# A routed feed-forward tail for short experts: rounded and rest columns side by side in one stationary operand

## The chip, the cores and the metric

The kernel runs on one core of a Trainium2 chip. The metric is the device time of one execution in microseconds, the median of several runs. Engines are named as the profile names them: PE is the matrix engine, PEld its weight load, DVE the vector engine, ACT the scalar engine, POOL the GpSimd engine, SP the engine that only issues transfers here. A name with a q behind it (DVEq, PEldq) is an engine's sequencer, which reads the program, branches and waits on semaphores.

## The reference

Three layers follow each other on 1536 tokens of 512 features. First local attention with pooled keys, then a dense feed-forward layer with 2048 hidden features, then the part that the change touches: eight experts of 1024 hidden features, of which each token uses one, up to 384 tokens for an expert.

```python
logits = x @ w_gate
expert_idx = np.argmax(logits, axis=1)
...
h = np.maximum(np.einsum('ecd,edf->ecf', disp, w1), 0.0)
y = np.einsum('ecf,efd->ecd', h, w2)
...
        out[i] = gate_w[i] * y[expert_idx[i], pos[i]]
```

Worked out from the reference with its own random seed, the experts get 880, 425, 168, 62 and 1 tokens, sorted by number; three experts get none.

## The kernel before

Attention and the dense layer take the first 370 us and are one long straight program. Then the experts run, sorted by their number of tokens, largest first; k is the place in that order. How many tokens each one has is known only while the kernel runs, so every engine loads the count into a register (count, line 1331) and branches on it.

Tokens are handled in blocks of 128. Experts with two or three blocks run through many_blocks; with one block through single (line 1353), which calls one_block (line 703). By the counts above k = 0 takes three blocks (the first is a special one), k = 1 three, k = 2 two, and k = 3 and k = 4 one block each. The places k = 3 and k = 4 are what this case is about.

Every matrix product is done in a 32-bit format with a shortened mantissa, and the lost part is made good: an operand is kept as a rounded value and the rest (its difference from the exact value), and a product is the sum of three passes, rounded by rounded, rounded by rest of the weights, rest by rounded weights (PASSES, line 662). In one_block the tokens are the stationary operand (128 columns) and 512 columns of weights move. The first layer is two halves of four chunks, so 2 x 4 x 3 = 24 matmuls (Block.first, line 671); ACT takes the positive part; PE turns the result by four 128x128 transposes per half (Block.turn, line 681), ACT and DVE make its rounded and rest parts; the second layer is 8 x 3 = 24 matmuls (Block.second, line 695); finish (line 646) scales by the gate and POOL scatters the rows to the output.

While a block runs, the weights of the next expert come in. They are 16 chunks of 256 KB. SP loads a chunk into one of eight raw buffers (raw_load, line 602); conv_hi (line 606) casts it to the rounded part, on ACT, or on DVE for chunks 2, 5, 8, 11 and 14; conv_lo (line 615) subtracts to get the rest, on DVE, or on POOL for those five chunks, and then lets SP load the chunk eight places on into the freed buffer. So chunk 15 can be loaded only when chunk 7 is converted. The call more(n) places the conversion of the next n chunks at that place of the program; each engine works its instructions off in program order, so a conversion that waits for its transfer holds up what stands behind it on that engine. In one_block the calls are 2, 3, 1, 1, then one after each of the second-layer steps 2 to 6, and what is left, four chunks, after finish. At step 4 ahead turns the next expert's gathered tokens (load_xT, line 637).

The branches around it are small (line 1378) for places with at most one block and large (line 1391) for the others. The code of the last alternative stands far behind that of the first, and what is not taken is jumped over.

## Time and profile before

| what | value |
|---|---|
| time, three runs | 508.5, 509.41 and 511.25 us, median 509.41 |
| the profiled execution's own time | 508.64 us |
| its span, first to last instruction | 506.9 us |
| mean granted PE clock | 0.981 |
| busy share of the span: PE, DVE, ACT, POOL | 93%, 64%, 54%, 37% |
| k = 3, first matmul to last (read from the timeline) | 472.36 to 485.22 us |
| k = 4, first matmul to last | 485.06 to 497.88 us |
| last scatter issued, end | 499.18, 506.9 us |

A matmul's row gives its start and a modelled end, and matmuls overlap: one of 512 columns is shown with some 0.39 us, while a row of them starts one every 0.23 to 0.24 us. The busy share of the whole span says little about the two short blocks, which are 5% of it; there the order of events is read from the timeline. A wait that is put down to "issue" is one for which the profile shows no cause; the rows of the sequencers around it show whether the engine was at a branch.

### The profile page before, as it was taken

The page shows a single profiled execution, that of the slowest core. Times are in us where ns is not written, and L with a number is a line of the kernel's source. Part 1 is how long each engine was busy: PE and PEld are TensorE (multiplying, and loading weights), DVE is VectorE, ACT ScalarE, POOL GpSimd, SP SyncE. Part 2 cuts the span into 40 slices and gives each one's busy share as a digit, 9 for nine tenths or more (in the row PEclk, how much of TensorE's full clock was granted, in tenths as well). Part 3 has the DMA queues.
Part 4 walks back from the last instruction along what each step waited for, and adds up shares of the span by engine and source line. Part 5 has one row for each costly group of instructions (what it writes and reads, how often), then busy time and mean ns, then how long its engine had stood idle before and what let it go on. Part 6 is the DMA issues. An engine that isn't in the chain of part 4 may idle for free.

```text
span 506.9 us, 9236 instructions
## 1 busy us (share of the span) xinstructions
PE 472.0 (93%) x3052; PEld 406.9 (80%) x3052; DVE 325.6 (64%) x880; ACT 271.8 (54%) x681; POOL 189.3 (37%) x197
## 2 busy tenths in 40 slices
PE   7798798889999999999999999999998999999892
PEld 6586577678888889999999899888767989888672
DVE  4699999878877761111149889846686755556460
ACT  4755656666667646664333333334654865566550
POOL 4345575633333335883223233223335040030440
PEclk9988998999999999999999999999999999999997
DMA  8996656667777441439010010012645966458380
GB/s 237 283 255 185 191 162 189 214 207 245 227 230 219 126 142 46 125 118 345 37 62 2 0 63 0 2 63 88 200 129 151 345 211 222 135 164 278 105 292 15
DMA packets 45634, 79.97 MB, mean 158 GB/s; under 512 B 4604, under 2 KB 19196, under 8 KB 45552
## 3 DMA queue, kind: packets, MB, share of 16 engines
q1 hardware_dynamic: 43792, 73.83, 46.4%
q0 software_dynamic: 1760, 5.19, 3.4%
q8 instruction: 34, 0.56, 0.5%
q14 instruction: 48, 0.39, 0.2%
HBM read 65.29 MB, written 13.11 MB: 155 GB/s over the span
## 4 chain that ended last, share of the span: by engine, by line
PE 65%; DVE 15%; DMA 13%; issue 2%; ACT 2%; POOL 1%; SPq 0%; DVEq 0%; POOLq 0%
PE acc L426 23%; PE h L393 22%; DMA xgq<-x2d,gidx 10%; PE bh L750 6%; PE y L739 5%; DMA vt<-vT 2%; DVE t1i L375 2%; DVE t1i L372 2%; DVE t1o L375 1%; DMA xg<-x2d,gidx 1%; PE T L294 1%; DVE st L285 1%; DVE sc L272 1%; PE O L334 1%; DVE t1o L372 1%
## 5 line engine op out<-in xcount | busy, mean ns | idle before, releaser
L393 PE MATMUL h<-xT,Wi 128*128 128x384 f32 x768 | 152.8, 346 | 8.2 <-DVE e L404 6.6
L393 PEld LDWEIGHTS h<-xT,Wi 128*128 128x128 f32 x768 | 137.2, 192 | 16.5 <-DVE e L404 8.7
L426 PE MATMUL acc<-Wo,g 128*128 128x512 f32 x576 | 145.8, 397 | 1.0 <-POOL Wo L382 1.0
L413 POOL TENSOR_TENSOR g<-e,g 128x384 fp32r<-128x384 f32 x63 | 71.4, 1133 | 145.5 <-ACT g L409 129.9
L426 PEld LDWEIGHTS acc<-Wo,g 128*128 128x128 f32 x576 | 105.9, 188 | 21.7 <-POOL Wo L382 1.3
L404 DVE SCALAR_TENSOR_TENSOR e<-e,h 128x384 f32<-128x384 f32 x64 | 35.3, 551 | 77.3 <-ACT e L400 77.3
L399 ACT ACTIVATE e<-h 128x384 f32<-128x384 f32 x64 | 31.4, 491 | 65.4 <-PE h L393 61.8
L409 ACT CAST g<-e 128x384 fp32r<-128x384 f32 x64 | 32.8, 513 | 42.6 <-DVE e L404 42.6
L618 DVE TENSOR_TENSOR E<-rawq,E 128x512 fp32r<-128x512 f32 x70 | 46.7, 705 | 9.1 <-ACT E L608 8.0
L279 ACT ACTIVATE sc<-sc,st 128x120 f32<-128x120 f32 x96 | 36.8, 385 | 28.8 <-DVE st L272 28.6
L750 PE MATMUL bh<-xbq,E 128*128 128x256 f32 (+1 forms) x288 | 43.6, 303 | 2.7 <-ACT ysf L654 1.4
L608 ACT CAST E<-rawq 128x512 fp32r<-128x512 f32 x75 | 42.7, 617 | 6.2 <-DMA rawq<-wx 3.5
L750 PEld LDWEIGHTS bh<-xbq,E 128*128 128x128 f32 x288 | 41.3, 188 | 5.0 <-ACT ysf L654 1.6
L287 POOL TENSOR_TENSOR sc<-sc,st 128x360 f32<-128x360 f32 x32 | 29.6, 925 | 41.3 <-DVE st L286 20.1
L739 PE MATMUL y<-E,g 128*128 128x512 f32 x168 | 41.7, 393 | 0.0
L488 DVE CUSTOM_DVE_ANT_0 dot<-a,wgb 128x512 f32<-128x512 f32 x48 | 40.0, 887 | 0.0
L739 PEld LDWEIGHTS y<-E,g 128*128 128x128 f32 x168 | 30.6, 188 | 5.7
L400 ACT ACTIVATE e<-e 128x384 f32<-128x384 f32 x64 | 33.7, 526 | 2.0
L272 DVE CUSTOM_DVE_ANT_0 sc<-S,masks 128x120 f32<-128x120 f32 x96 | 21.5, 276 | 14.2 <-PE S L247 10.4
L758 DVE TENSOR_TENSOR g<-e,g 128x256 fp32r<-128x256 f32 (+1 forms) x24 | 11.3, 469 | 23.8 <-ACT g L757 23.6
L655 POOL DMA_INDIRECT out<-ys,sidx x6 | 6.3, 1053 | 47.4 <-ACT ys L654 46.0
L755 ACT ACTIVATE e<-bh 128x256 f32<-128x256 f32 (+1 forms) x24 | 10.1, 419 | 22.4 <-PE bh L750 22.4
(225 smaller groups left out, 634.5 us busy)
## 6 DMA issues: line engine op xcount, KB each, us to landing
rawq<-wx SPq DMA_DIRECT2D x88, 256.0 KB, 4.3
rawi<-wi SPq DMA_DIRECT2D x16, 512.0 KB, 5.0
rawo<-wo SPq DMA_DIRECT2D x16, 512.0 KB, 5.5
vw<-vP SPq DMA_DIRECT2D x16, 288.0 KB, 6.7
kt<-kT SPq DMA_DIRECT2D x8, 400.0 KB, 5.6
qt<-qT SPq DMA_DIRECT2D x16, 192.0 KB, 5.9
vt<-vT SPq DMA_DIRECT2D x8, 384.0 KB
out<-xg SPq DMA_DIRECT2D x12, 256.0 KB, 3.6
```

Source lines behind the costliest of these rows:

```text
L279: nc.scalar.activation(out=sc[:, gi], in_=sc[:, gi], func=AF.Exp, bias=st[:, 0, gi : gi + 1], scale=-1.0, accum_out=st[:, 1, gi : gi + 1])
L393: nc.tensor.matmul(HP[t, f][:, 0:TT], lhsT=w[:, s, c * P : (c + 1) * P], rhs=xT[t][:, xs, c, :], start=c == 0 and n == 0, stop=c == NCC - ...
L400: nc.scalar.activation(out=e, in_=e, func=AF.Relu, bias=1.0, scale=-1.0)
L404: nc.vector.scalar_tensor_tensor(out=e, in0=e, scalar=-1.0, in1=h[:, 0:TT], op0=ALU.mult, op1=ALU.max)
L409: nc.scalar.copy(gT[t, f][:, 0], EP[t, f])
L413: eng.tensor_tensor(g[:, 1], EP.pop((t, f)), g[:, 0].bitcast(F32), op=ALU.subtract)
L426: nc.tensor.matmul(accp[tb], lhsT=g[:, s, tb * P : (tb + 1) * P], rhs=w[:, ws], start=f % FPG == 0 and n == 0, stop=f % FPG == FPG - 1 and ...
L488: nc.vector.tensor_tensor_reduce(out=junk, in0=x2[t * BPT + tb], in1=WGB[e // 2][:, e % 2], scale=1.0, scalar=0.0, op0=ALU.mult, op1=ALU.a ...
L608: (nc.vector.tensor_copy if m in vec else nc.scalar.copy)(EW[k][m][:, 0], raw_of(k, m))
L618: (nc.gpsimd if m in pool else nc.vector).tensor_tensor(w[:, 1], raw, w[:, 0].bitcast(F32), op=ALU.subtract)
L739: nc.tensor.matmul(ys[b], lhsT=g[:, s, b * P : (b + 1) * P], rhs=w[:, ws], start=f == 0 and n == 0, stop=f == 7 and n == 2)
L750: nc.tensor.matmul(h[:, 0:nt], lhsT=EW[k][half * NCC + c][:, ws, fc * P : (fc + 1) * P], rhs=xb[:, s, c, 0:nt], start=n == 0, stop=n == 3 ...
```

## The change

An expert of at most 64 tokens gets its own block, tiny_block. Its tokens fill only half of the 128 stationary columns, so the rounded part goes into columns 0 to 63 and the rest part into columns 64 to 127 of one operand (pair_up, in a free third of the token buffer). Two passes over the weights, rounded and rest, then give rounded tokens by both weight parts in result rows 0 to 63 and rest tokens by both in rows 64 to 127; ACT copies the upper rows down and DVE adds the lower ones. The product is then 2 x 4 x 2 = 16 and 8 x 2 = 16 matmuls a block, and the transposes are of 64 columns. The second layer is scaled by a table of gates that is repeated for both halves of the rows (gate2), made by one small matmul after k = 0.

Core of the diff:

```diff
+        H = P // 2
+        def pair_up(k, j, *copy):
+            xb = XB[k % 2]
+            for s in range(2):
+                copy[s](xb[:, j, :, 2 * P + s * H : 2 * P + (s + 1) * H], xb[:, s, :, j * P : j * P + H])
+        class HalfBlock:
+            def __init__(self, k, j, nm, pair=True):
...
+                if pair:
+                    pair_up(k, j, nc.scalar.copy, nc.vector.tensor_copy)
...
+            def first(self, half, c):
...
+                for ws in range(2):
+                    nc.tensor.matmul(self.h[half], lhsT=self.xb[:, c], rhs=w[:, ws],
+                                     start=c == 0 and ws == 0, stop=c == NCC - 1 and ws == 1)
+                if c == NCC - 1:
...
+                    nc.scalar.copy(e[0][0:H], h[H:P])
+                    nc.vector.tensor_tensor(e[1][0:H], h[0:H], e[0][0:H], op=ALU.add)
...
+            def turn(self, half):
...
+                nc.scalar.activation(out=g[:, :, 0], in_=hv, func=AF.Relu)
+                nc.vector.scalar_tensor_tensor(
+                    out=g[:, :, 1], in0=hv, scalar=0.0, in1=g[:, :, 0].bitcast(F32), op0=ALU.max, op1=ALU.subtract)
...
+            def end(self, j):
...
+                nc.scalar.mul(out=ys[0:H], in_=self.y[H:P], mul=gate2[H:P, e : e + 1])
+                nc.vector.scalar_tensor_tensor(
+                    out=ys[0:H], in0=self.y[0:H], scalar=gate2[0:H, e : e + 1], in1=ys[0:H],
+                    op0=ALU.mult, op1=ALU.add)
...
+        def tiny_block(k, nm, head, more, ahead):
+            blk = HalfBlock(k, 0, nm, head)
+            more(2)
+            for c in range(NCC):
+                blk.first(0, c)
+            more(1)
+            for c in range(3):
+                blk.first(1, c)
+            blk.turn(0)
+            blk.first(1, 3)
+            more(1)
+            blk.second(0)
+            blk.second(1)
+            blk.turn(1)
+            more(1)
+            for f in range(2, 8):
+                blk.second(f)
+                if f == 4 and ahead():
+                    pair_up(k + 1, 0, nc.gpsimd.tensor_copy, nc.gpsimd.tensor_copy)
+                if f < 7:
+                    more(1)
+            blk.end(0)
+            more(NCHUNK)
...
+        def tiny(k, head=True):
...
+            nxt = count(k + 1)
+            with tc.If(nxt > 0) as c:
+                tiny_block(k, nm, head, *fetch(k + 1, nm, 1, range(2, NCHUNK, 3)))
+                tiny(k + 1, False)
+            with c.Else():
+                tiny_block(k, nm + "z", head, *fetch(NE, "", 1, ()))
...
         def small(k, cv):
             with tc.If(cv > 0):
-                if k + 1 == NE:
...
+                with tc.If(cv < H + 1) as d:
+                    tiny(k)
+                with d.Else():
...
         first_expert(cv0, min(GRP, nj - 1))
+        pt = psm("twice", "T")
+        nc.tensor.matmul(
+            pt[:, 0 : n2 * NE], lhsT=twice.rearrange("p a q -> p (a q)"), rhs=once, start=True, stop=True)
+        nc.vector.tensor_copy(gate2, pt[:, 0 : n2 * NE])
         large(1, cv1)
```

Three places of the program show what moves. The first is DVE at the head of k = 3, from the branch on its count to the first additions; names beginning with E are the next expert's weight chunks by number, rawq the raw buffers, hT the turned hidden values, xbq the token buffers. Before:

```order
L1380 COMPARE_AND_BRANCH
L1331 TENSOR_LOAD regs
L1385 COMPARE_AND_BRANCH
L618 TENSOR_TENSOR E_0_3995<-rawq_3983,E_0_3995 128x512
L618 TENSOR_TENSOR E_1_3996<-rawq_3984,E_1_3996 128x512
L608 CAST E_2_3997<-rawq_3985 128x512
L618 TENSOR_TENSOR E_3_3998<-rawq_3986,E_3_3998 128x512
L618 TENSOR_TENSOR E_4_3999<-rawq_3987,E_4_3999 128x512
L693 TENSOR_TENSOR hT_3_0_10563<-ht_3_0_10601,hT_3_0_10563 128x512
```

And with the change (te is the sum of the two result halves, g the operand of the second layer):

```order
L1489 COMPARE_AND_BRANCH
L1490 COMPARE_AND_BRANCH
L1428 TENSOR_LOAD regs
L1481 COMPARE_AND_BRANCH
L708 COPY xbq_4378<-xbq_4378 128x4x64
L618 TENSOR_TENSOR E_0_3995<-rawq_3983,E_0_3995 128x512
L618 TENSOR_TENSOR E_1_3996<-rawq_3984,E_1_3996 128x512
L731 TENSOR_TENSOR te_3th<-th_3th,te_3th 64x512
L608 CAST E_2_3997<-rawq_3985 128x512
L742 SCALAR_TENSOR_TENSOR g_3th<-tt_3th,g_3th 128x4x64
L731 TENSOR_TENSOR te_3th<-th_3th,te_3th 64x512
L618 TENSOR_TENSOR E_3_3998<-rawq_3986,E_3_3998 128x512
```

One more branch stands ahead, and a copy that PE's first matmul needs now stands first on DVE; chunks 3 and 4, ahead of the first turned values before, stand behind the work of both halves.

The second place is DVE from the conversion of chunk 6 to the end of k = 3. Before, chunk 7 is converted ahead of the next expert's tokens (xbq_4377):

```order
L618 TENSOR_TENSOR E_6_4001<-rawq_4453,E_6_4001 128x512
L693 TENSOR_TENSOR hT_3_0_10564<-ht_3_0_10628,hT_3_0_10564 128x512
L618 TENSOR_TENSOR E_7_4002<-rawq_4454,E_7_4002 128x512
L608 CAST E_8_4003<-rawq_3983 128x512
L644 TENSOR_TENSOR xbq_4377<-bt_4_3_0_10650,xbq_4377 128x4x128
```

And with the change, behind them:

```order
L618 TENSOR_TENSOR E_6_4001<-rawq_4453,E_6_4001 128x512
L644 TENSOR_TENSOR xbq_4377<-bt_4_3th,xbq_4377 128x4x128
L618 TENSOR_TENSOR E_7_4002<-rawq_4454,E_7_4002 128x512
L608 CAST E_8_4003<-rawq_3983 128x512
L618 TENSOR_TENSOR E_9_4004<-rawq_3984,E_9_4004 128x512
```

So the conversion that frees the buffer of chunk 15 moved behind a step that waits for PE's second-layer step 4.

The third place is the way from k = 3 to k = 4 with the change, on DVE; the row behind the branch is jumped over here:

```order
L608 CAST E_14_4009<-rawq_4453 128x512
L618 TENSOR_TENSOR E_15_4010<-rawq_4454,E_15_4010 128x512
L1428 TENSOR_LOAD regs
L1481 COMPARE_AND_BRANCH
L618 TENSOR_TENSOR E_0_4463<-rawq_3983,E_0_4463 128x512
```

The branch asks whether k = 5 has tokens. As it has none, DVE jumps over 143 instructions (counted in the built program; PE over 275, ACT over 96, POOL over 82) to k = 4's block, whose first work on DVE is the sum te of its first half. Before, this way led over a jump of 7 and one of 34 instructions on DVE. At the very end before, each engine jumped twice (DVE over 106 and 562, PE over 311 and 1523); now once, over 3108 and 6732.

## Rows read from the trace of the kernel before

**Rows 1.** Stretches of the tail: length; PE, PEld, DVE, ACT, POOL busy; clock; DMA
```profile
470.00:472.30 2.30, 0.36 (x2) 0.00 (x0) 0.48 (x1) 0.47 (x1) 1.62 (x2) 1.00 0.32 118
472.30:485.00 12.70, 12.64 (x60) 10.11 (x61) 8.13 (x13) 7.20 (x13) 6.10 (x5) 1.00 0.55 158
485.00:498.00 13.00, 12.49 (x57) 9.59 (x56) 6.05 (x10) 4.68 (x9) 4.16 (x3) 1.00 0.64 217
```

**Rows 2.** Timeline, entry to k = 3: start, duration, instruction, idle before it
```profile
472.36 4.45 PE L676 MATMUL bh<-E,xbq 128*128 128x512 f32 x18 [2.00 <-issue]
...
475.50 1.29 DVE L618 TENSOR_TENSOR E<-rawq,E 128x512 fp32r<-128x512 f32 x2 [4.11 <-ACT E L608]
```

**Rows 3.** DVE's branches out of k = 2 (L1396) and into k = 3 (L1380)
```profile
L1396 DVEq COMPARE_BRANCH  x1: 74/74/74, 470.9 to 470.9; - x1
...
L1380 DVEq COMPARE_BRANCH  x1: 50/50/50, 474.8 to 474.8; - x1
```

**Rows 4.** Groups by shape on PE, k = 3: count, busy us, mean ns
```profile
L700 PE MATMUL y<-E,hT 128*128 128x512 f32 x24 | 6.4, 405 | 0.0
...
L684 PE MATMUL ht<-ident,hs 128*128 128x128 f32 x8 | 1.2, 272 | 0.0
```

**Rows 5.** Groups by shape that stand for the added operations
```profile
L679 ACT ACTIVATE hs<-bh 128x512 f32<-128x512 f32 x2 | 1.2, 599 | 1.7 <-PE bh L676 1.7
L693 DVE TENSOR_TENSOR hT<-ht,hT 128x512 fp32r<-128x512 f32 x2 | 1.4, 686 | 0.5 <-ACT hT L686 0.5
L758 DVE TENSOR_TENSOR g<-e,g 128x256 fp32r<-128x256 f32 x16 | 6.8, 425 | 10.1 <-ACT g L757 10.0
L197 POOL COPY kw<-kt 128x192 f32<-128x192 f32 x3 | 1.0, 343 | 2.5 <-DMA kt<-kT 2.5
```

**Rows 6.** Chunks 7 and 15: conversion of 7, load of 15, its landing and conversion
```profile
481.88 0.68 DVE L618 TENSOR_TENSOR E<-rawq,E 128x512 fp32r<-128x512 f32 x1
...
483.18 0.33 SPq L604 DMA_DIRECT2D rawq<-wx  x1
...
488.33 0.62 ACT L608 CAST E<-rawq 128x512 fp32r<-128x512 f32 x1 [0.70 <-DMA rawq<-wx]
489.00 0.67 DVE L618 TENSOR_TENSOR E<-rawq,E 128x512 fp32r<-128x512 f32 x1
...
DMA to landing us min/median/max: 2.7/3.5/4.3
```

**Rows 7.** Branches: PE in k = 2, DVE into k = 4, both at the end
```profile
L1401 PEldq COMPARE_BRANCH  x2: 1054/2036/3017, 441.8 to 443.5; - x2
...
L1385 DVEq COMPARE_BRANCH  x2: 47/54/62, 489.0 to 490.1; - x2
...
L1380 PEldq COMPARE_BRANCH  x2: 3797/4264/4732, 495.1 to 499.3; - x2
L1380 DVEq COMPARE_BRANCH  x2: 47/52/56, 498.4 to 499.2; - x2
L1380 DVEq EVENT_SEMAPHORE  x2: 21/21/21, 498.9 to 499.1; - x2
```

**Rows 8.** PE early in the kernel at either clock, and the clock of a stretch
```profile
52.45 2.35 PE L393 MATMUL h<-xT,Wi 128*128 128x384 f32 x12 [1.53 <-DVE e L404]
60.81 3.91 PE L393 MATMUL h<-xT,Wi 128*128 128x384 f32 x12 [2.11 <-DVE e L404]
...
61.20:64.60 3.40, 3.40 (x13) 3.30 (x12) 3.40 (x5) 1.62 (x4) 2.69 (x2) 0.50 1.01 290
```

**Rows 9.** The end: scaling, last scatter, POOL's last branches and drain
```profile
469.00 0.69 ACT L654 ACTIVATE ys<-y,gate 128x512 f32<-128x512 f32 x1 [1.98 <-PE y L739]
...
497.91 0.47 ACT L651 ACTIVATE ys_0z<-y_0z,gate 128x256 f32<-128x256 f32 x1 [3.61 <-PE y_0z L700]
499.18 1.01 POOL L655 DMA_INDIRECT out<-ys_0z,sidx x1 [8.37 <-DVEq L1380]
L1380 POOLq COMPARE_BRANCH  x2: 38/44/50, 499.7 to 500.9; - x2
```

More of the change, by code (lines that the diff above doesn't have):

```diff
@@ L1265, in ahead @@
                 load_xT(XB[k % 2], i * P, XG[i], f"{i}_{k}" + nm)
+            return True
         GS = {0: slots(tf0.rearrange("p (j v) -> p j v", v=3), nj, "a") + (0,)}
@@ L1328, in build @@
         finish(blk.y, st["slot0"][0][:, 0:1], st["slot0"][1][:, 0:1], "f", ysf)
+        n2 = min(nj, 2)
+        twice = bpool.tile([P, 2, H], F32, name="twice")
+        nc.gpsimd.tensor_copy(twice, ident[:, 0:H].unsqueeze(1).to_broadcast([P, 2, H]))
+        once = bpool.tile([P, n2 * NE], F32, name="once")
+        for j in range(n2):
+            nc.gpsimd.tensor_copy(
+                once[:, j * NE : (j + 1) * NE], allsl[0].rearrange("p (e j) -> p j e", j=nj)[:, j])
+        gate2 = bpool.tile([P, n2 * NE], F32, name="gate2")
         def count(k):
@@ L1376, in others @@
                     one_block(k, XB[k % 2], *slots_of(k, [j]), f"_{k}_{j}o", lambda n: None, lambda: None)
+        def tiny(k, head=True):
+            nm = f"_{k}t" + "h" * head
+            if k + 1 == NE:
+                tiny_block(k, nm, head, *fetch(NE, "", 1, ()))
+                return
+            nxt = count(k + 1)
[4 more added lines that the diff above has]
+                tiny_block(k, nm + "z", head, *fetch(NE, "", 1, ()))
         def small(k, cv):
             with tc.If(cv > 0):
-                if k + 1 == NE:
-                    single(k, 0, None)
-                    return
-                nxt = count(k + 1)
-                with tc.If(nxt > 0) as c:
-                    single(k, 0, k + 1)
-                with c.Else():
-                    single(k, 0, None)
-                small(k + 1, nxt)
+                with tc.If(cv < H + 1) as d:
+                    tiny(k)
+                with d.Else():
+                    if k + 1 == NE:
+                        single(k, 0, None)
+                    else:
+                        nxt = count(k + 1)
+                        with tc.If(nxt > 0) as c:
+                            single(k, 0, k + 1)
+                        with c.Else():
+                            single(k, 0, None)
+                        small(k + 1, nxt)
         def large(k, cv):
```

30 lines of the change are left out of this document (added).

## The prediction

> **What bounds the kernel now.** The page says that PE is busy for 93% of the span, which invites the thought that fewer matmuls make the kernel faster in proportion. The change touches two blocks, k = 3 and k = 4, so I read these alone: first the stretches, then the timeline around the entry to k = 3, then the groups by shape, last the branches and the transfers. The stretches show PE idle for nearly all of 470.0 to 472.3 and then full in both blocks, 12.64 of 12.70 us and 12.49 of 13.00 us [rows 1]. So the blocks are bound by PE as they stand, but the entry is bound by something else: PE's first matmul at 472.36 follows 2.00 us with no cause shown, and DVE's first work starts only at 475.50 [rows 2]. The reader should see why: DVE leaves k = 2 by a branch at 470.9 and reaches the next one at 474.8 [rows 3], 3.9 us for one jump over 814 instructions (counted in the built program). PE is through its own jump three microseconds earlier and needs nothing of DVE for a while. That slack hides DVE's late entry. It is the first thing that the change spends.
>
> The second bound stands just behind PE: the weights of k = 4. Chunk 15 can be loaded when chunk 7 is converted (the subtraction at 481.88), its load goes out at 483.18, ACT's cast of it waits for the transfer and starts at 488.33, DVE's subtraction at 489.00 [rows 6]. ACT's and DVE's work for k = 4 stands behind these in the program. PE has 18 matmuls of k = 4 to do meanwhile, so this shows as only a few tenths of a wait.
>
> **The change, part by part.** Times continue the profiled execution's own clock.
>
> *Fewer matmuls.* 18 matmuls take 4.45 us [rows 2], the last one's own 0.4 among them, so one starts every 0.235 us or so. 16 fewer in each block are 3.8 us less of PE's work a block, 7.5 us in all. This is gained only where PE is what others wait for.
>
> *The head of k = 3.* PE's first matmul now needs both halves of pair_up, one of them a copy on DVE. DVE is free at 475.50 at the earliest [rows 2]; one more branch is 0.1 us, the copy of 256 elements takes under the 0.43 us of a two-input operation of that size [rows 5], I take 0.3. PE starts at 475.95 instead of 472.36: 3.6 us lost. If DVE came as early as PE does today, nothing would be lost here; that end is a rival below.
>
> *Inside k = 3.* Each half now has a chain that PE waits for: 8 matmuls (1.9 us, 0.2 until ACT sees the result), ACT's copy of the upper rows (512 elements, 0.60), DVE's addition (0.69) [rows 5]; the transposes start at 479.45, and PE has 6 matmuls to cover this, nearly enough. Then transposes (0.15 each [rows 4]), the positive part and the rest (256 elements, 0.43 each [rows 5], with 0.1 between engines): the second layer starts 1.65 us later, at 481.1, behind two matmuls only. After it come 16 matmuls, 8 transposes and 0.3 us of waiting for the second half, 4.9 us. PE is done at 486.0 instead of 485.2 (today's 24 second-layer matmuls alone take 6.4 us [rows 4]). So k = 3 itself takes 10.0 instead of 12.9 us, and ends 0.8 us later because it began 3.6 later.
>
> *The weights of k = 4.* DVE subtracts chunk 7 now behind the next tokens, which wait for PE's transposes at second-layer step 4 (done at 484.6), ACT's cast (0.25 and 0.60) and DVE's own subtraction (0.69). Chunk 7 is done at 486.9 instead of 482.56, and the load of chunk 15 goes out at 487.2 instead of 483.18 [rows 6]: 4.0 us later. Landing takes 2.7 to 4.3 us, median 3.5, and up to the 5.15 us between that load and the cast which waits for it [rows 6]; with fewer loads crowded together I take 3.5, so 490.7. ACT's cast (0.62) and DVE's subtraction (from 491.4) follow. Only behind these do ACT copy and DVE add for k = 4. POOL's two copies for k = 4's operand (some 0.4 us each by its 0.34 for 192 elements [rows 5], behind a conversion of 1.3 us) come at 487.5 and are not last.
>
> *The jump to k = 4.* DVE must first jump over 143 instructions. The nearest rows: DVE's jump over 106 took 0.45 us (498.4 to the event at 498.9) and the one over 814 took 3.9 [rows 3, 7]; PE's jumps over 155, 181 and 311 took 1.05, 3.02 and 3.80 [rows 7]. I take 1.0, nearest to the 155, and keep 0.45 and 3.9 as ends. With loading the count (DVE's branch, load and branch took 1.1 us at this place, 489.0 to 490.1 [rows 7], one branch fewer now) the addition starts at 493.15. PE's own jump over 275 costs 3.0 to 3.8 us, from some 2.5 us ahead of its last matmul (its branch at 495.1 stands that far ahead today [rows 7]); it is through by 487.9 and is not last.
>
> [...]
>
> *Inside k = 4.* From the addition (0.8 to the transposes) the same 6.1 us follow as in k = 3 without the token transposes: y is seen at 500.25. Scaling was split over two engines (0.47 us each); now ACT scales one half of the rows at 512 elements (0.69 [rows 9]) and DVE adds the other (0.69), in series: the scatter goes out at 502.0 instead of 499.18 [rows 9]. That is **+2.8 us**.
>
> *PE's clock.* Before k = 3 PE now idles from 470.4 [rows 1] to 475.95, and in k = 4 about 3 us for DVE. [...] Today's 2.00 us entry left it at 1.00 [rows 1], so it does not always fall. [...] I take 1.4 for the first, whose idling is more than twice as long, and half of it for the second: **+2.1 us**, between 0 and 3.1.
>
> *The rest.* At the end each engine jumps once instead of twice. POOL's two branches stand 1.2 us apart [rows 9]; it gains between 0 and that, **-0.6**. The small matmul and copy for gate2 after k = 0 lie beside a wait of 0.5 us on PE; POOL's three small copies are covered by its idling in k = 0: **+0.1**, at most 0.3. If that cover were gone they would cost some 1 us.
>
> Sum: 2.8 + 2.1 - 0.6 + 0.1 = 4.4 us, on the profiled execution's own 508.64 us (span 506.9 and 1.7 around it): 513.0. That execution stands 0.8 us below the median of the three runs, 509.41, which spread over 2.75 us. I forecast **513.0 us**, 0.7 to 0.9% slower.
>
> **The rivals.**
>
> *Kind fetches and an untouched clock.* DVE's jump costs 0.45 and the clock never falls: 508.64 + 2.8 - 0.55 - 0.6 + 0.1 = 510.4, no change that shows. For it speak DVE's short jumps, against it the 5.6 us of idle PE.
>
> *A long fetch on DVE.* The jump over 143 misses as the one over 814 did: 2.9 us more, 515.9. For it speak PE's 3.02 us at 181; against it DVE's 0.45 at 106.
>
> *PE's saving wins (faster).* If DVE were through the entry when PE is, 3.5 us earlier, k = 3 would start at 472.5 and end at 482.5; if in addition chunk 15 landed early enough for k = 4's chain, k = 4 would take its 10 us and the scatter go out near 494: about 503.5. It decides at DVE's entry: for each microsecond that DVE comes before 475.5, the rest moves up by one, and the time falls below that of today from some 2.5 us on, with the clock held. Against it: DVE's far jump stays, and is no shorter for the added code [rows 3], and chunk 15 still follows chunk 7.
>
> *The block is not taken.* If the chip's routing gave the fourth expert more than 64 tokens, only branches are added: 508.7. The count is 62 by the reference, so this needs three tokens routed otherwise.
>
> **How the numbers follow.** Forecast 0.50 (its own range 511.2 to 515.5; 0.04 of it under 512.0), long fetch 0.16, kind fetches 0.24, faster 0.05, not taken 0.05. A measurement of this kernel can tell about 0.5%, 2.5 us, from no change. Slower by more: 0.46 + 0.16 = 0.62. Faster by more: 0.05. Within: 0.33. The range 508.4 to 517.0 takes in the kind and the untaken case below, and above the long fetch with a crowded landing (515.9 and some 1.1); it leaves out the faster rival and the worst sums, together under 0.2.
>
> **What would show it.** Right: L725's first matmul at 475.5 to 477.5, its wait ended by DVE L708; chunk 15's cast waiting for its transfer around 490 to 492; PE idle for some 3 us in k = 4, ended by DVE L731; a stretch at 0.50 after 474; the last scatter near 504. Wrong: L725 starting by 473; DVE L731 of k = 4 not waiting behind chunk 15; a last scatter before 500.

## The result and the profile after

The changed kernel takes 513.76 us (median of 21 runs, 509.68 to 517.13) beside 510.0 us for the kernel before (507.29 to 513.94, run on the same chip). The ratio is **1.0076, 95% interval 1.0052 to 1.0101**: slower by about 3.9 us, where 513.0 us had been forecast. The ratios here compare undisturbed runs alone and are not the quotient of the two medians beside them; the two can differ by some 0.3%.

The profiled execution has its own time of 515.87 us, a span of 514.2 us and a clock of 0.968; that is 7.2 us above the profiled one of before, so this execution shows more than the typical loss, and a second profile follows below. Up to the end of k = 2 the kernels agree: ACT's last scaling there (L651) starts at 470.14, before at 470.40. The whole difference lies behind it.

The stretches of the tail (length; PE, PEld, DVE, ACT, POOL busy; granted clock; DMA share; GB/s) show it first:

```profile
475.00:482.00 7.00, 6.75 (x19) 4.93 (x20) 2.33 (x5) 0.63 (x2) 2.12 (x2) 0.55 0.36 114
...
494.50:497.50 3.00, 0.07 (x1) 0.07 (x2) 2.67 (x4) 1.09 (x2) 1.26 (x1) 1.00 0.89 281
497.50:501.00 3.50, 3.23 (x12) 1.88 (x12) 1.11 (x2) 0.97 (x2) 0.00 (x0) 0.63 0.81 284
501.00:506.50 5.50, 5.23 (x16) 3.81 (x16) 0.42 (x1) 0.62 (x2) 0.00 (x0) 0.61 0.03 7
```

PE, full and at 1.00 all the way before [rows 1], now stands idle for 3 us in k = 4, and its clock is granted at 0.50 over 475.2 to 481.2 and again over 498.5 to 504.5. Both had been forecast. What the reader should not pass over is the first row's DVE: busy for 2.33 of 7.00 us, in the very stretch in which it has the weights of k = 4 to convert.

The timeline of the entry to k = 3:

```profile
473.45 0.41 ACT L708 CAST xbq<-xbq 128x256 fp32r<-128x256 f32 x1 [2.84 <-issue]
...
474.81 0.29 DVE L708 CAST xbq<-xbq 128x256 fp32r<-128x256 f32 x1 [3.68 <-issue]
...
475.25 6.28 PE L725 MATMUL th_3th<-E,xbq 128*128 128x512 f32 x14 [5.15 <-DVE xbq L708]
```

PE starts 5.11 us behind the end of k = 2 instead of 1.96 [rows 2], released by DVE's copy, and its 14 matmuls take 6.28 us; before, 18 took 4.45.

DVE's own rows from there to k = 4's first addition, on DVE's timeline:

```profile
475.02 1.29 DVE L618 TENSOR_TENSOR E<-rawq,E 128x512 fp32r<-128x512 f32 x2
479.70 0.68 DVE L731 TENSOR_TENSOR te_3th<-th_3th,te_3th 64x512 f32<-64x512 f32 x1 [3.39 <-ACT te_3th L730]
...
482.37 0.42 DVE L742 SCALAR_TENSOR_TENSOR g_3th<-tt_3th,g_3th 128x256 fp32r<-128x256 f32 x1 [1.65 <-ACT g_3th L741]
...
487.84 0.94 DVE L618 TENSOR_TENSOR E<-rawq,E 128x512 fp32r<-128x512 f32 x1
...
495.04 1.74 DVE L618 TENSOR_TENSOR E<-rawq,E 128x512 fp32r<-128x512 f32 x1 [0.20 <-ACT E L608]
496.70 0.67 DVE L731 TENSOR_TENSOR te_4tz<-th_4tz,te_4tz 64x512 f32<-64x512 f32 x1
```

Two chunks are subtracted, then DVE waits 3.39 us for ACT's copy of the upper rows, then 1.65 us for the positive part. In the kernel before, DVE had subtracted five chunks and cast two more by the time it first waited, for 0.47 us. The waits of DVE between 474.5 and 497 (what waited, on what, us in all, times, longest):

```profile
DVE te_3th L731 <- ACT te_3th L730: 3.9, 2, 3.4
DVE xbq L708 <- issue: 3.7, 1, 3.7
DVE g_3th L742 <- ACT g_3th L741: 2.0, 2, 1.6
```

So DVE stands still for 5.9 us behind the new block's own chain, beside 0.5 us behind hT before (and a 0.9 us wait for the next tokens, now 0.2). Chunk 7 (487.84) is subtracted 17.70 us behind the end of k = 2, before 11.48 [rows 6]. What that does to chunk 15 (POOL, SP, ACT):

```profile
486.60 1.63 POOL L618 TENSOR_TENSOR E<-rawq,E 128x512 fp32r<-128x512 f32 x1 [4.47 <-PE bt_3th L640]
...
488.26 1.48 SPq L604 DMA_DIRECT2D rawq<-wx  x3
...
494.39 0.62 ACT L608 CAST E<-rawq 128x512 fp32r<-128x512 f32 x1 [2.71 <-DMA rawq<-wx]
```

SP issues in order: the load of chunk 13 waits for POOL's subtraction of chunk 5 (486.60 and 1.63), and 14 and 15 stand behind it. The third of these three issues, chunk 15's, starts at 489.40, 19.3 us behind the end of k = 2 (before 12.8 [rows 6]); its cast follows at 494.39.

The end of k = 4:

```profile
497.43 0.46 PE L737 MATMUL tt_4tz<-ident,te_4tz 64*128 64x64 f32 x4 [3.92 <-DVE te_4tz L731]
...
498.83 2.07 PE L749 MATMUL ty_4tz<-E,g_4tz 128*128 128x512 f32 x4 [0.27 <-DVE g_4tz L742]
...
501.45 4.78 PE L749 MATMUL ty_4tz<-E,g_4tz 128*128 128x512 f32 x12
...
506.27 0.68 ACT L756 ACTIVATE ys_4tz<-ty_4tz,gate 64x512 f32<-64x512 f32 x1 [4.33 <-PE ty_4tz L749]
...
508.00 0.91 POOL L760 DMA_INDIRECT out<-ys_4tz,sidx  x1 [11.77 <-POOLq L1481]
```

PE waits 3.92 us for DVE's addition, which stands behind chunk 15. From the scatter to the end it is 6.2 us instead of 7.7 [rows 9], more than the 0.6 us forecast for one jump instead of two. DVE's jump into k = 4, branch and first event behind it:

```profile
L1481 DVEq COMPARE_BRANCH  x1: 69/69/69, 495.4 to 495.4; - x1
...
L731 DVEq EVENT_SEMAPHORE  x1: 21/21/21, 496.0 to 496.0; - x1
```

It took 0.48 us at most (ACT's copy, for which the event waits too, ended at 495.87): the short of the two ends that the prediction had kept.

### The profile page after: what moved, and what is told of

It is laid out like the page before. It is cut to its first block, busy times and chain, and to the rows that moved or that the text cites. A ratio compares the mean times of both kernels' runs of the same rounds, so it can differ in the third digit from the quotient of the medians.

```text
span 514.2 us, 9172 instructions
## 1 busy us (share of the span) xinstructions
PE 470.7 (92%) x3022; PEld 404.0 (79%) x3022; DVE 329.1 (64%) x886; ACT 271.7 (53%) x682; POOL 191.5 (37%) x202
## 3 DMA queue, kind: packets, MB, share of 16 engines
q0 software_dynamic: 1696, 5.19, 3.2%
## 5 line engine op out<-in xcount | busy, mean ns | idle before, releaser
L393 PEld LDWEIGHTS h<-xT,Wi 128*128 128x128 f32 x768 | 137.0, 191 | 16.7 <-DVE e L404 9.0
L279 ACT ACTIVATE sc<-sc,st 128x120 f32<-128x120 f32 x96 | 36.8, 386 | 28.9 <-DVE st L272 28.8
L618 DVE TENSOR_TENSOR E<-rawq,E 128x512 fp32r<-128x512 f32 x70 | 48.7, 736 | 3.6 <-ACT E L608 2.4
L272 DVE CUSTOM_DVE_ANT_0 sc<-S,masks 128x120 f32<-128x120 f32 x96 | 21.5, 277 | 14.6 <-POOL g L413 5.8
L655 POOL DMA_INDIRECT out<-ys,sidx x5 | 5.0, 1009 | 46.7 <-ACT ys L654 45.4
L842 ACT ACTIVATE e<-bh 128x256 f32<-128x256 f32 (+1 forms) x24 | 10.1, 420 | 23.3 <-PE bh L837 19.7
```

The costliest lines, as they stand in the source:

```text
L279: nc.scalar.activation(out=sc[:, gi], in_=sc[:, gi], func=AF.Exp, bias=st[:, 0, gi : gi + 1], scale=-1.0, accum_out=st[:, 1, gi : gi + 1])
L393: nc.tensor.matmul(HP[t, f][:, 0:TT], lhsT=w[:, s, c * P : (c + 1) * P], rhs=xT[t][:, xs, c, :], start=c == 0 and n == 0, stop=c == NCC - ...
L618: (nc.gpsimd if m in pool else nc.vector).tensor_tensor(w[:, 1], raw, w[:, 0].bitcast(F32), op=ALU.subtract)
```

## The experiments

The parts of the program ahead of k = 3 differ by some microseconds from one execution to the next (k = 2 ends between 468.65 and 474.30 in the profiles below), so the positions in this table are counted from the start of ACT's last scaling of k = 2 in the same profile. The ratios are to the kernel before, from timed runs on the same chip. "Near" is the first real matmul of k = 3, "addition" the first of k = 4. Each position is that of a single execution and does not have to follow the ratio: e3, e5 and e8 end alike, at 38.9 to 39.0 us, with ratios of 1.0069, 1.0044 and 1.0008.

| kernel | ratio, 95% interval | near | addition | last scatter | end |
|---|---|---|---|---|---|
| before | 1 | 1.96 | none | 28.8 | 36.5 |
| changed | 1.0076, 1.0052 to 1.0101 | 5.11 | 26.6 | 37.9 | 44.1 |
| changed, again | 1.0081, 1.0049 to 1.0112 | 5.19 | 24.2 | 33.8 | 40.6 |
| e1, not taken | 1.0388, 1.0332 to 1.0443 | 6.75 | none | 42.6 | 54.1 |
| e2, early pair | 1.0115, 1.0069 to 1.0162 | 2.01 | 24.4 | 34.4 | 40.6 |
| e3, PE kept busy | 1.0069, 1.0036 to 1.0103 | 5.12 | 23.9 | 32.5 | 39.0 |
| e4, k = 3 alone | 1.0177, 1.0128 to 1.0226 | 5.13 | none | 35.4 | 43.0 |
| e5, defer | 1.0044, 1.0020 to 1.0067 | 5.12 | 24.0 | 32.5 | 39.0 |
| e6, fewer loads | 1.0054, 1.0024 to 1.0083 | 5.14 | 25.6 | 34.1 | 40.9 |
| e7, pair and defer | 1.0012, 0.9985 to 1.0039 | 3.04 | 21.2 | 29.8 | 37.1 |
| e8, order | 1.0008, 0.9973 to 1.0043 | 5.39 | 24.0 | 32.6 | 38.9 |
| e9, all three | 1.0013, 0.9979 to 1.0047 | 3.07 | 22.2 | 31.0 | 37.2 |
| e10, copies and fill | 1.0025, 0.9998 to 1.0053 | 3.08 | 21.0 | 33.1 | 39.6 |
| e11, near block last | 1.0032, 1.0009 to 1.0055 | 3.72 | 19.5 | 32.0 | 38.3 |

**The changed kernel again.**

> The changed kernel once more, unchanged, as the reference for the other runs of this group and for a second profile. By my theory the waits repeat (PE into k = 3 behind DVE's copy, DVE's addition of k = 4 behind chunk 15), with k = 4's addition some 26 us behind the end of k = 2, while the falls of the clock may differ: ratio to the kernel before 1.004 to 1.011. If the first profile's 7.5 us was the whole effect and no chance of the clock, the ratio is 1.012 or more.

Measured: 514.05 beside 509.8 us, ratio 1.0081. The waits repeat, with the addition at 24.2 us and not at the 26 expected. This profile's tail is 4.1 us longer than before's, as much as the ratio says, and it is used below as the nearer to the typical case; the first profile's was longer by another 3.4 us. By their own times the two lie 2.0 us below and 2.1 us above their medians. Two rows of the second:

```profile
474.96 4.83 PE L725 MATMUL th_3th<-E,xbq 128*128 128x512 f32 x14 [5.22 <-DVE xbq L708]
...
493.97 0.68 DVE L731 TENSOR_TENSOR te_4tz<-th_4tz,te_4tz 64x512 f32<-64x512 f32 x1
```

With as much idling ahead (5.22 and 5.15 us) the same 14 matmuls took 4.83 and 6.28 us, at a granted clock of 0.70 and 0.50 over 475 to 480: how long PE's clock stays low varies from one execution to the next here.

**e1, the block not taken.**

```diff
-                with tc.If(cv < H + 1) as d:
+                with tc.If(cv < 1) as d:
```

> The branch on 64 tokens is changed to one on 0 tokens, so no expert takes the new block; all its code, gate2 and the extra branches stay in the program. If the loss comes from the late operand, the clock and chunk 15, it is gone: 508.5 to 510.5 us, ratio to the kernel before 0.998 to 1.002, PE enters k = 3 after some 2.0 us of idling and is granted 1.00 there. If the larger program itself costs (longer jumps), the time stays at 512 or more, and PE's and DVE's jumps into k = 3 are longer than the 3.9 us of DVE before.

Measured: 528.08 beside 509.41 us. This is the second case, and far beyond its bound: 3.9% slower, although no expert takes the new block. The branch over the new code, in front of k = 3 and again of k = 4, on three engines (count, duration min/median/max in ns, first and last start), and PE's entry to k = 3:

```profile
L1490 PEldq COMPARE_BRANCH  x2: 4880/4932/4983, 472.3 to 489.7; - x2
L1490 ACTq COMPARE_BRANCH  x2: 50/50/50, 473.9 to 495.1; - x2
L1490 DVEq COMPARE_BRANCH  x2: 63/63/63, 475.5 to 495.8; - x2
...
477.87 6.25 PE L676 MATMUL bh<-E,xbq 128*128 128x512 f32 x18 [6.80 <-issue]
```

One jump over the new block and all that is nested in it costs PE 4.9 us. DVE's, to its next instruction at 479.4, took 3.8 us, not longer than the 3.9 of before, so that half of the expectation failed. The slow 18 matmuls (6.25 us, before 4.45) are in the loss too; how it divides is not shown. The jump isn't a price of having the code: the changed kernel falls through here. But an input whose short experts have 65 to 128 tokens would meet such jumps. The rival that the block is not taken was put at 508.7 us, as if the added branches cost nothing; by this run that price was far off.

**e2, the operand pair made early.**

```diff
-                if f == 5:
-                    ahead()
+                if f == 5 and ahead() and nb == 2 and k + 1 < NE:
+                    pair_up(k + 1, 0, nc.gpsimd.tensor_copy, nc.gpsimd.tensor_copy)
...
-                    tiny(k)
+                    tiny(k, k != 3)
```

> POOL makes the paired operand of k = 3 already inside k = 2, where it idles, so PE's first matmul of k = 3 no longer waits for DVE (for the counts of this input; the general case of a third block is left out). Theory of the late operand: PE starts at 472.3 to 473.0 instead of 475.25, its clock stays at 1.00 over the first 4 us, k = 3 ends 4 to 6 us earlier, and since DVE's subtraction of chunk 7 stands behind the next tokens, chunk 15 lands 2 to 4 us earlier too: 508 to 511 us, 0.988 to 0.994 of the changed kernel. Rival, DVE's own late entry sets the conversions and so the end: PE starts early but chunk 15's cast moves by under 1 us and the time stays at 512.5 to 514.

The copy runs in k = 0 too and overwrites part of k = 1's third block there, which changes values and not the work. Measured: 513.66 beside 509.41 us, ratio 1.0115: no gain. PE did start early, and still nothing came of it. The entry, and DVE's jump into k = 4:

```profile
471.87 5.04 PE L725 MATMUL th_3t<-E,xbq 128*128 128x512 f32 x14 [2.05 <-issue]
...
L1481 DVEq COMPARE_BRANCH  x1: 69/69/69, 490.5 to 490.5; - x1
...
L731 DVEq EVENT_SEMAPHORE  x1: 21/21/21, 494.2 to 494.2; - x1
```

Three things are to be seen. The clock fell after 2.05 us of idling (0.61 granted over 472 to 476), where it had held at 1.00 after 2.00 in the kernel before. DVE was at its branch 20.6 us behind the end of k = 2, 2.9 us earlier than in the second profile of the changed kernel (23.5 us). And its jump took 3.64 us instead of at most 0.5, which gave that back (ACT's copy had ended at 491.22 and was not what the addition waited for). The long jump, a rival that the changed kernel itself had escaped, met its repair.

**e3, PE kept busy.**

```diff
             blk = HalfBlock(k, 0, nm, head)
+            if head:
+                busy(18)
...
+            if not head:
+                busy(22)
             blk.turn(0)
```

> PE is given 18 unused transposes at the head of k = 3 and 22 in k = 4 ahead of its first turn, to fill the two idle stretches; nothing else changes. If the clock is a cost of its own, the granted clock stays at 1.00 from 475 to 482 and from 497 to 506, the first 14 matmuls of k = 3 take 3.3 to 3.6 instead of 6.3 us, those of k = 4 behind the wait some 2.5 us less, and the time falls by 2.5 to 5.5 us: 508.5 to 511. Rival, the waits for DVE and chunk 15 set the end and the slow matmuls lie beside them: the clock is up but the time falls by under 1.5 us, 512.5 or more.

Measured: 512.26 beside 509.41 us, ratio 1.0069; the changed kernel has 1.0076 and 1.0081. The clock was kept at the entry (first row). The other rows are POOL's subtraction of chunk 5, chunk 15's load, k = 4's first matmuls and chunk 15's cast:

```profile
479.40:482.90 3.50, 3.44 (x14) 2.54 (x14) 1.78 (x4) 0.58 (x1) 0.98 (x1) 1.00 0.52 163
...
488.07 1.63 POOL L618 TENSOR_TENSOR E<-rawq,E 128x512 fp32r<-128x512 f32 x1 [3.45 <-PE bt_3th L640]
...
490.88 0.33 SPq L604 DMA_DIRECT2D rawq<-wx  x1
...
491.64 5.00 PE L725 MATMUL th_4tz<-E,xbq 128*128 128x512 f32 x14 [2.19 <-POOL xbq L708]
...
495.91 0.62 ACT L608 CAST E<-rawq 128x512 fp32r<-128x512 f32 x1 [2.81 <-DMA rawq<-wx]
```

14 matmuls in 3.44 us, and k = 3 itself took 10.0 us (479.42 to 489.45), as forecast. The addition of k = 4 came 2.7 us earlier than in the first profile, where the clock had been low longest, and 0.3 us earlier than in the second. The time moved by 0.1% at most on the ratios' middles, and their intervals leave room for some 2 us; the 2.5 to 5.5 us expected are not there. That is nearer to the rival. But the run is no clean test of a kept clock: in front of k = 4 PE idled 2.19 us and the clock fell there instead, 14 matmuls taking 5.00 us (0.76 granted over 492 to 498) where both profiles of the changed kernel have 3.52. With the clock kept at the entry chunk 15's load left 16.6 us behind the end of k = 2, earlier than in either profile of the changed kernel (19.3 and 18.0).

**e4, k = 3 alone in the new block.**

```diff
-                tiny(k + 1, False)
+                small(k + 1, nxt, False)
...
```

> Only k = 3 takes the new block; k = 4 goes through the old block with three passes. If the entry (late operand and clock) is the larger part of the loss, it stays, and the old block of k = 4 hides chunk 15 behind its 18 first matmuls again: 511 to 514 us, a scatter some 2 to 4 us later than in the kernel before. If the new block of k = 4 is the larger part (its chain behind chunk 15, its own fall of the clock), the time is 508.5 to 510.5.

Measured: 517.51 beside 509.41 us, outside both expectations. With the old block in k = 4 the kernel is slower than with the new one. That speaks against the new block of k = 4 as the place of the loss but does not show it, and the run can't price it: the nested branches differ too, and POOL idles 6.16 us ahead of its gather at the entry instead of 4.04.

**e5, three chunks converted later.**

```diff
+            late = list(late)
+            def old(n):
+                for m in late[:n]:
+                    conv_expert(k, [m], range(2, NCHUNK, 3), range(2, NCHUNK, 3))
+                del late[:n]
...
                 blk.first(0, c)
+            old(1)
             more(1)
...
             blk.first(1, 3)
+            old(1)
             more(1)
...
             blk.turn(1)
+            old(NCHUNK)
...
-            more(NCHUNK)
+            more(NCHUNK - 10 - keep)
```

> The conversions of the last three chunks (13, 14, 15) move from the end of k = 3 into k = 4's own block, behind its first addition, its second addition and its second turn; all results are the same. Theory, chunk 15 sets k = 4: ACT and DVE are through their jump when PE's eight matmuls end, the addition starts near 492.5 instead of 496.7 on the first profile's clock, PE idles under 1.5 us there, and the time falls by 3 to 6 us, ratio to before 0.993 to 1.001. Rival, DVE and POOL are busy with conversions all the way, so that the same work only moves: the time falls by under 1.5 us. Rival, the wait moves to the last second-layer step: PE idles there for chunk 15 and the gain is 1 to 3 us.

Measured: 512.39 beside 509.8 us, ratio 1.0044: about 1.9 us of the 4.1 are gone by the middles of the ratios, but the intervals overlap. That is the size of the third case and not its mechanism: the last 12 matmuls of k = 4 ran without a wait, in 3.13 us. DVE reached its branch at 490.5, 20.0 us behind the end of k = 2 (23.5 in the changed kernel), and then its jump, lengthened to 159 instructions by the moved code, took 3.8 us.

**e6, the loads that nobody uses.**

```diff
-                elif 0 < k < NE - 1:
+                elif 0 < k < 4:
```

> The loads of weights for k = 5, which SP issues while k = 4's chunks 8 to 15 are converted and which nobody uses here, are left out (an input with more experts in use would need them). If chunk 15 lands late because it shares the DMA engines with them, it lands in under 3.5 instead of 5.5 us and the addition of k = 4 starts 1.5 to 3 us earlier, ratio to before 1.000 to 1.004. If its 5.5 us come from the loads ahead of it, nothing moves but the DMA share behind 494: within 0.3% of the changed kernel.

Measured: 513.4 beside 509.8 us, ratio 1.0054; its interval overlaps with that of the changed kernel in the same group, so a gain isn't shown. Chunk 15's load (the third of three) and its cast:

```profile
485.76 1.48 SPq L604 DMA_DIRECT2D rawq<-wx  x3
...
492.18 0.62 ACT L608 CAST E<-rawq 128x512 fp32r<-128x512 f32 x1 [2.93 <-SPq L1481]
```

With nothing issued behind it the chunk still took 5.3 us from its issue (486.91) to the cast, and 4.5 to 5.0 us in the two profiles of the changed kernel. So the loads behind it are not shown to slow its landing. (The profile puts the end of this wait down to SP's branch; what else held the cast is not shown.)

**e7, early pair and later chunks together.** The pair is made in a free gather buffer whenever tokens are turned:

```diff
-                copy[s](xb[:, j, :, 2 * P + s * H : 2 * P + (s + 1) * H], xb[:, s, :, j * P : j * P + H])
+                copy[s](pair()[:, :, s * H : (s + 1) * H], XB[k % 2][:, s, :, 0:H])
...
-                if pair:
-                    pair_up(k, j, nc.scalar.copy, nc.vector.tensor_copy)
...
                 load_xT(XB[k % 2], i * P, XG[i], f"{i}_{k}" + nm)
+            if k:
+                pair_up(k, nc.gpsimd.tensor_copy, nc.gpsimd.tensor_copy)
```

> Both repairs together: the last three chunks converted in k = 4's block as before, and the paired operand always made by POOL when the tokens are turned, in a free gather buffer, so that no block has copies at its head; all results are the same. If the two waits, at the entry and at chunk 15, are what the change pays for its 16 matmuls fewer per block, the two gains add: PE enters k = 3 at 2.0 to 2.3 us of idling and k = 4's last scatter stands 28 to 30.5 us behind the end of k = 2, where the kernel before has 28.8; ratio to before 0.985 to 0.998. Rival, the conversions for k = 4 can't be done sooner than in the kernel before, since DVE enters k = 3 as late as ever: ratio 0.999 to 1.005 in spite of both.

Measured: 510.39 beside 509.8 us, ratio 1.0012: no loss can be shown any more, and no gain. The ratio lies in the rival's range and not in the first. The scatter at 29.8 us is inside the range expected, but PE's first matmul followed 3.07 us of idling instead of 2.0 to 2.3. That row, and DVE's jump, which was long here too:

```profile
475.41 5.04 PE L725 MATMUL th_3th<-E,xgq 128*128 128x512 f32 x14 [3.07 <-DMA out<-ys,sidx]
...
L1493 DVEq COMPARE_BRANCH  x1: 69/69/69, 489.8 to 489.8; - x1
...
L731 DVEq EVENT_SEMAPHORE  x1: 21/21/21, 493.5 to 493.5; - x1
```

ACT's copy, for which the addition waits, had ended at 492.21, so 1.4 us of k = 4 hang on the jump.

**e8, the order of the conversions.** One number:

```diff
             blk = HalfBlock(k, 0, nm, head)
-            more(2)
+            more(5)
```

> The changed kernel with one number of its block changed: five chunks of the next expert are converted at its head instead of two, as in the old block, which calls two and three ahead of its first wait. In the changed kernel DVE stands still for 5 to 6 us between 476 and 483 behind ACT's copy and positive part while loaded chunks wait. Theory, DVE's conversions set when k = 4 can go on: chunk 7 is subtracted some 2.5 to 3.5 us earlier behind the end of k = 2 (17.7 us in the first profile, 16.5 in the second), the addition of k = 4 follows 2 to 3 us earlier (24.2 in the second profile), ratio to before 1.001 to 1.005 against 1.008 for the changed kernel. Rival, the transfers set it: chunk 15's cast waits for its transfer as long as before, and the time stays within 0.2% of the changed kernel. Rival, the first addition of k = 3, now behind five chunks, delays PE by as much as is gained: no change either, with PE's idling ahead of the first turn over 2 us.

Measured: 511.66 beside 509.72 us, ratio 1.0008, interval 0.9973 to 1.0043; both intervals of the changed kernel lie above it. DVE's waits, the load of chunk 15 and the first matmuls of k = 4:

```profile
DVE te_4tz L731 <- ACT te_4tz L730: 2.2, 1, 2.2
DVE g_3th L742 <- ACT g_3th L741: 1.0, 2, 0.6
DVE te_3th L731 <- ACT te_3th L730: 0.8, 2, 0.5
...
485.89 0.33 SPq L604 DMA_DIRECT2D rawq<-wx  x1
...
490.35 4.84 PE L725 MATMUL th_4tz<-E,xbq 128*128 128x512 f32 x14 [2.65 <-issue]
```

DVE's standing still behind k = 3's chain fell from 5.9 and 4.6 us (first and second profile of the changed kernel) to 1.8. Chunk 7 was subtracted 14.6 us behind the end of k = 2 instead of 17.7 and 16.5, chunk 15's load left at 15.3 instead of 19.3 and 18.0, its cast came at 19.7 instead of 24.3 and 22.5. So the theory holds up to there. But the addition came at 24.0, hardly ahead of the 24.2 of the second profile: it now waits for PE, whose jump into k = 4 took 4.5 us and whose first 14 matmuls then took 4.84 us, at a granted clock of 0.71 over 490.3 to 495.4. That part of the expectation, 2 to 3 us earlier, failed: with chunk 15 out of the way the next wait stood right behind it. So the run shows that this number lowers the loss, and not by which way. The profile ends 1.7 us earlier than the second one of the changed kernel; 0.2 of that is the addition, 1.0 lies between the addition and the scatter, where PE's clock was kept this time (the second layer's first four matmuls in 1.20 us instead of 2.06), and 0.5 behind the scatter. Nor is the loss shown to be gone: the interval leaves up to 2.2 us, the medians alone differ by 1.9, and this profile's tail is 2.4 us longer than before's.

**e9, all three repairs.** e7 with two chunks instead of one at three places:

```diff
                 blk.first(0, c)
             old(1)
-            more(1)
+            more(2)
...
-            more(1)
+            more(2)
             blk.second(0)
...
             old(NCHUNK)
-            more(1)
+            more(2)
...
-            more(NCHUNK - 10 - keep)
+            more(NCHUNK - 13 - keep)
```

> All three repairs: operand pairs made by POOL when the tokens are turned, chunks 13 to 15 converted in k = 4's block, and two chunks instead of one at three places of the block; all results are the same. If DVE's order of work is the bound that is left, the last scatter stands 27.5 to 29 us behind the end of k = 2 (28.8 in the kernel before, 29.8 with the first two repairs): ratio to before 0.993 to 0.999, the change pays for the first time, by 0.5 to 3.5 us. If DVE's sum of work is the bound (its conversions take the same time wherever they stand), it stays at 0.999 to 1.003.

Measured: 511.66 beside 509.72 us, ratio 1.0013. No gain over e7 or e8.

```profile
487.33 5.04 PE L725 MATMUL th_4tz<-E,xgq 128*128 128x512 f32 x14 [3.02 <-POOL xgq L710]
```

PE had idled 3.02 us in front of k = 4, its 14 matmuls took 5.04 us as with a fallen clock, and the addition waited for them. The ratio is that of the second case, the scatter at 31.0 us is outside the first, but the trace shows neither of their causes: DVE waited 3.50 us for ACT's copy behind PE's late and slow start, so DVE's sum of work was not what bound there.

**e10, two details, and e11, the other order of the two alternatives.**

```diff
             blk = HalfBlock(k, nm)
+            if head:
+                busy(8)
...
-                pair_up(k, nc.gpsimd.tensor_copy, nc.gpsimd.tensor_copy)
+                pair_up(k, *(nc.scalar.copy, nc.vector.tensor_copy) if "t" in nm else [nc.gpsimd.tensor_copy] * 2)
```

> The three repairs, with two details more: inside k = 3 the operand pair of k = 4 is copied by ACT and DVE (0.41 and 0.29 us) instead of POOL (1.40 us, for which PE waits 1.2 us), and PE gets 8 unused transposes at the head of k = 3, where it waits 0.8 us in the run before; all results are the same. If PE's start into k = 4 and its clock are what is left, k = 4's first matmul follows the end of k = 2 by 16.3 to 16.8 us instead of 17.6, the last scatter by 29 to 30.3 instead of 31.0, ratio to before 0.994 to 0.9995. Rival, PE's jump into k = 4 sets its start and the clock falls there as before: the scatter stays at 30.5 to 31.5 and the ratio at 0.999 to 1.003.

```diff
-            with tc.If(nxt > 0) as c:
+            with tc.If(nxt < 1) as c:
+                tiny_block(k, nm + "z", head, *fetch(NE, "", 1, ()), late)
+            with c.Else():
...
-            with c.Else():
-                tiny_block(k, nm + "z", head, *fetch(NE, "", 1, ()), late)
```

> The same, with the two alternatives of the short block in the other order: the block with no expert behind it stands first, so that k = 4 is reached without a jump and k = 3 by one jump over that block. If the jump into k = 4 (3.8 to 4.5 us on PE, hidden in part) is what PE waits for, k = 4's first matmul comes 1 to 2 us earlier than in the run beside it and PE idles under 1 us there, so that its clock is kept and 14 matmuls take 3.5 instead of 5.0 us: ratio to before 0.988 to 0.997. Rival, the jump at the head of k = 3, with nothing to hide it, costs each engine what is gained: within 0.3% of the run beside it.

Measured: 511.59 and 512.1 us beside 509.63, ratios 1.0025 and 1.0032: the rivals' side both times. In e10 k = 4's first matmul came at 16.5 us, as aimed at, but the clock fell there (14 matmuls in 5.05 us behind 1.88 us of idling) and the scatter came at 33.1, later than either case. In e11 that matmul came no earlier (16.7 us, behind 1.86 us of idling), so the jump was not what it waited for; only the clock was kept. And in both a wait that no expectation had named stood behind it:

```profile
488.13 3.51 PE L725 MATMUL th_4tz<-E,xgq 128*128 128x512 f32 x14 [1.86 <-DVE xgq L710]
...
495.31 0.58 ACT L730 COPY te_4tz<-th_4tz 64x512 f32<-64x512 f32 x1 [2.69 <-DMA out<-ys_3th,sidx]
```

PE kept its clock (14 matmuls in 3.51 us, 1.00 granted over 488 to 492) and the first addition of k = 4 came 4.7 us earlier than in the changed kernel's second profile. Then ACT waited 2.69 us (2.42 in e10) for k = 3's scatter to be read out. The block takes five buffers of one kind (two additions with a copy each, and the result) out of three, and the second copy of k = 4 falls on the buffer that k = 3's scatter reads. Whether the block beats the old one with another buffer there was not tried. No kernel here is shown to be faster than the kernel before.

## Why the prediction came out

The sign, the size (513.0 against 513.76) and the places of the waits were right. The reasons were right only in part, and the terms missed in both directions, so that the nearness of the two numbers is partly luck.

*Head of k = 3: size right, weight not shown.* PE started 3.2 us later than before, by DVE's copy, as worked out (3.6). That this is passed on to the end was read from PE's chain. In e2, with PE on time, DVE came to its jump 2.9 us earlier, so the step does reach DVE; the time did not fall, as the jump in that program was 3.1 us longer. That this is why it did not fall is read from one profile, in which the clock fell as well; what the entry alone is worth stays open.

*Inside k = 3: right with the clock held.* 10.0 us forecast, 10.0 in e3; 12.7 and 11.4 in the two profiles of the changed kernel, where the clock fell.

*The weights of k = 4: the load in time with the clock held, the landing too short.* The forecast has chunk 15's load at 487.2, which is 16.8 us behind the end of k = 2. It left at 16.6 in e3, and at 19.3 and 18.0 in the two profiles of the changed kernel. So 2.7 and 1.4 us of its lateness go with the slow matmuls at the head of k = 3, behind which DVE stands still for 5.9 and 4.6 us, in e3 for 3.2: the clock, counted as a term of its own, comes in by this way as well. The agreement with e3 is partly luck. The prediction had chunk 7 behind the next tokens as the cause; in the traces the load of chunk 13 waits for POOL's subtraction of chunk 5, which is late because DVE casts chunk 5 late, and the loads of 14 and 15 follow in SP's order. Behind that is the order of the conversions at the block's head: one_block calls two and three chunks ahead of its first wait, the new block two and one. The prediction had both orders before it and did not price the difference; e8 puts five there, and the load leaves at 15.3. The landing was mis-sized: 3.5 us were taken, and from the load to the cast that waited for it passed 5.0, 4.5 and 5.0 us (both profiles, e3). That is why the cast, a sign set at 490 to 492, came at 494.39 and 492.26 with the late load.

*The jump to k = 4: at either end, never between.* 1.0 us was taken between 0.45 and 3.9. It took at most 0.48 and 0.53 us in the changed kernel, and 3.6 to 3.8 us in e2, e5 and e7, whose code differs by some instructions. So the rival of the long jump (in the prediction a long fetch) was rightly kept: the changed kernel escaped it, three of its neighbours did not. What DVE does in a long jump no run shows, only its time.

*PE's clock: too small as an event, not shown as a cost.* No run shows the 1.4 us that the sum takes for the first fall, nor the half of it for the second; they are the author's estimates. In their place the runs have these: the first fall cost up to 6.28 - 3.44 = 2.8 us of PE's time (1.4 in the second profile), the second 2.8 us in the first profile (the second layer of k = 4 went from 498.83 to 506.2, 7.4 us with the transposes in it, where e3 needed 4.65). By the tails of single profiles the falls go with 5.1 and 1.6 us (44.1 and 40.6 beside e3's 39.0). Yet in the timed runs e3 gains less than can be measured, with a fall of its own in k = 4, and e8, which has a fall in front of either block (14 matmuls in 5.14 and in 4.84 us), has the smaller loss. How much of the 2.1 us in the sum is really paid stays open between nothing and some 2 us.

*The end and gate2: right.* From the scatter to the end 1.5 and 0.9 us less (forecast 0.6), and gate2 cannot be seen: in both profiles k = 2 ends no later than before.

So the total was right, and its terms partly cancelled. Without its clock term the forecast has a tail of 36.5 + 2.8 - 0.6 + 0.1 = 38.8 us; e3's is 39.0. In it the landing took some 1.5 us more than forecast and chunk 15's subtraction 1.0 (1.70 us), while the jump, of which nothing lay between that subtraction and the addition, cost some 1.1 less, PE's start 0.4 and the end some 0.6 less. What is shown is where the waits stand and that the order of the conversions moves chunk 15 and lowers the loss. How the 3.9 us divide between the late conversions, the late entry and the clock is not shown: one profile of each kernel was taken, two of the changed one.

## What to carry to other kernels

When a block is made shorter, carry over where its background work stands, not only what it computes: where a wait holds up the ready work behind it, as on DVE here (5.9 us of standing still, 0.5 before), each wait of the new chain should have as much ready work in front of it as the old chain had. Follow each of the added dependent steps to the engine that also does the background work, and ask how long that engine stands still, before asking what PE saves. And where a program branches, treat a jump as a cost that an edit elsewhere in the code can change by some 3 us (0.5 and 3.7 us here), and look first at the jump that an engine has no other work to hide.

## What the runs showed of the hardware that was not expected

**DVE's jump into k = 4 took 0.5 or 3.7 us.** It spans 121 to 160 instructions. Counted from DVE's first instruction in the built programs, its targets stand at 2741 (e6) and 2872 (both profiles of the changed kernel and e3), where it took at most 0.48 to 0.53 us, and at 2895, 2900 and 2901 (e2, e5, e7), where it took 3.64, 3.83 and 3.69. What sets the two apart no run shows.

**A jump over the whole new block** (e1) cost PE 5.0, ACT 3.9 and DVE 3.8 us in front of k = 3. In front of k = 4 it cost PE 4.9 us again, but DVE, over 162 instructions by the same count, was at its next instruction within 0.5 us. DVE's next instruction behind either branch (475.5 and 495.8):

```profile
L1428 DVEq TENSOR_LOAD <-regs x1: 326/326/326, 479.4 to 479.4; - x1
...
L1428 DVEq TENSOR_LOAD <-regs x1: 745/745/745, 496.3 to 496.3; - x1
```

**The clock is no function of the idling alone.** At the entry to k = 3 it held after 2.00 us (before: 18 matmuls in 4.45 us) and fell after 2.05 (e2: 14 in 5.04); in front of k = 4 it held after 2.02 (changed kernel: 14 in 3.52) and 1.86 (e11: 3.51) and fell after 1.82 (e7: 5.05) and 1.88 (e10: 5.05); and after 5.15 and 5.22 us the same 14 matmuls took 6.28 and 4.83 us.

**DVE's subtraction took longer beside POOL's.** In the tails of the kernel before, the changed kernel and e8 each one with no subtraction of POOL beside it took 0.67 to 0.69 us, and those beside one for more than 1 us took 1.60 to 2.22; with a shorter overlap some were as fast as alone. The one at 495.04, beside POOL's from 494.97, took 1.74 us, right ahead of the addition of k = 4. In the tail of the changed kernel the eleven of them take 0.96 us on the mean, before 0.77.
